# Where TensorE waits for transferred rows: on the scores that read them, or on fill products a slot or two ahead

## The chip, the cores and the metric

The kernel runs on one core of one Trainium2 chip. The metric is the device time of one execution in microseconds; lower is better. A time is the median of several runs, and one further execution was profiled.

## What is computed

An input x of 2048 tokens by 512 features is normalised, goes through sliding-window attention (32 heads of 16 features, each query sees itself and the 255 keys before it) and through an MLP with a gate, and the two are joined:

```python
xn = layernorm(x)
qkv = xn @ wqkv                                   # 32 heads of 16
scores = (q @ k.T) * 16 ** -0.5, masked to 0 <= i - j < 256
s = (softmax(scores) @ v) @ wo
h = gelu(layernorm(xn) @ w1 + b1)                 # 1792 wide
g = silu(h @ w2 + b2)
out = x + s * g
```

Everything is in float32; products are built from a rounded high part and a low remainder of each operand, three products for one.

## The kernel before, in words

The attention part is a hand-written pipeline of **slots**. One slot t handles one block of 128 queries or keys of one group n of four heads; there are 8 groups of 16 blocks, so t runs from 0 to 127, with a few slots ahead of 0 for the start. A slot has two halves. In each, TensorE first makes the probabilities' scores of one pair of heads into the one tile `stb` (`prob_block`), which ScalarE then raises into `pt`; `stb` may be written again only when ScalarE has read it. Between the two halves stand other products: the scores of a block 12 slots ahead, used only for the row maxima (`max_block` into `xy`, `first_scores` into `zo`), the product of probabilities and values (`pv_step`, `zo<-pt,vt`), and **fill products**: single matmuls of other stages (`fb<-xnT,wqb` and the like) that the tables `fills` deal out to the slots.

Scores read `slots[n % 2]` (tiles `qk0`, `qk1`), which hold the query and key rows of a group in a layout that matmuls cannot write. So a fill stage computes 512 columns (a chunk c of group n) into the bank `fb`, ScalarE copies it to `pjr` and rounds it to `sh`, GpSimd subtracts for the low part, and SyncE's queue carries the rows into the slot tile: four transfers of `sh`, two of `pjr`, from group 2 on one more (`copy_rows`, called by `send`, `send_high` and `send_low` in `job_qk` and `pair_qk`). The row maxima of four blocks go the same way through HBM (`max_rows`; the last step, `bring_in`, is `qk<-mT_d`).

`tandem(t0, t1, one, two)` deals out the fill products of two such stages over slots t0 to t1, in pairs that sit on the two row halves of the array; each `unit` is one pair, and it returned nothing. `fill_in(t, half)` runs what is due in a half slot. All engines but SyncE keep program order, so what stands behind a waiting matmul on TensorE waits too. Which semaphores a matmul waits for was left to the tile framework: the first reader of a tile waits for all the transfers into it, so the first score of a chunk carried up to eight waits.

Of the kernel before, what the change touches and what calls it, by code (L numbers as in the profile page):

```python
# [9 lines left out]
F32 = mybir.dt.float32  # L10
# [8 lines left out]
P = 128  # L19
# [9 lines left out]
ORDER = mybir.DependencyInfo(mybir.DependencyClass.Sync, mybir.DependencyReason.DATA)  # L29
# [21 lines left out]
def mixer_kernel(ctx, tc, x, wqk, wv, wo, w1, b1, w2, b2, out):  # L51


    nc = SimpleNamespace(**{name: Ordered(tc, name) for name in ("tensor", "vector", "scalar", "gpsimd", "sync")})
# [16 lines left out]
        (eng or nc.scalar.copy)(dst_hi, src)  # L71
        nc.vector.tensor_sub(dst_lo, src, dst_hi.bitcast(F32))

    def copy_rows(dst, src):
        nc.sync.dma_start(dst.bitcast(F32), src.bitcast(F32))

    def load(pool, tag, src, name, shape=(P, 512)):
        t = pool.tile(list(shape), F32, tag=tag, name=name)
# [81 lines left out]
    def run(steps):  # L160
        for step in steps:
            step()
# [11 lines left out]
    slots = []  # L174
# [126 lines left out]
    def job_qk(n, c):  # L301

        box = []
        ops = [(kt, a, b) for kt in range(KT) for a, b in PASSES]
        if not n and c < 3:
            ops.sort(key=lambda o: o[2])
        sl = slice(512 * c, 512 * (c + 1))

        def mm(i):
            if i == 0:  # L310
                box.append(fill_bank() if n or c else xy[:, 0])
            kt, a, b = ops[i]
            nc.tensor.matmul(box[0], wqs[n][:, a, kt], big[:, b, kt, sl],
                             start=(i == 0), stop=(i == len(ops) - 1))

        def send(src, qk, tt):
            copy_rows(slots[n % 2][tt:P:4, qk, :, sl], src[64 * qk: 64 * qk + 64])

        def finish():
            hi = sgp.tile([P, 512], F32R, tag="sh", name=f"sh_{n}_{c}", bufs=2)  # L320
            raw = t2.tile([P, 512], F32, tag="t2", name=f"pjr_{n}_{c}")
            lo = raw.bitcast(F32R)
            src = raw if n else box[0]
            if n:
                nc.scalar.copy(raw, box[0])

            def high():
                nc.scalar.copy(hi, src)
                behind(now[0], send_high)

            def send_high():
                for qk, tt in ((1, 0), (0, 0), (1, 2), (0, 1)):
                    send(hi, qk, tt)

            def low():
                (nc.gpsimd if n else nc.vector).tensor_tensor(lo, src, hi.bitcast(F32), op=ALU.subtract)
                behind(now[0], send_low)

            def send_low():
                send(lo, 1, 1)  # L340
                send(lo, 0, 2)

            later(1 if n else 0, high)
            later(3 if n else 1, low)
        return [(216, mm, i) for i in range(len(ops))], finish
# [17 lines left out]
    def pair_qk(n, c):  # L363

        ops = [(kt, a, b) for kt in range(KT) for a, b in PASSES]
        sl = slice(512 * c, 512 * (c + 1))

        def mm(ps, i, r, **flags):
            kt, a, b = ops[i]
            return nc.tensor.matmul(ps, wqs[n][r, a, kt], big[r, b, kt, sl], **flags)  # L370

        def send(src, qk, tt):
            copy_rows(slots[n % 2][tt:P:4, qk, :, sl], src[64 * qk: 64 * qk + 64])

        def finish(ps, t, copy):
            hi = sgp.tile([P, 512], F32R, tag="sh", name=f"sh_{n}_{c}", bufs=2)
            raw = t2.tile([P, 512], F32, tag="t2", name=f"pjr_{n}_{c}")
            lo = raw.bitcast(F32R)
            copy(raw, ps)

            def send_high():
                if n >= 2:
                    copy_rows(slots[n % 2][3:P:32, 0, :, sl], slots[n % 2][7:P:32, 0, :, sl])
                for i, (qk, tt) in enumerate(((1, 0), (0, 0), (1, 2), (0, 1))):
                    send(hi, qk, tt)
                    if i == 1 and (n, c) in among:
                        among[n, c]()

            def send_low():
                send(lo, 1, 1)  # L390
                send(lo, 0, 2)


            free = t if (n, c) == (1, 2) else max(t + 1 + 2 * (c % 2), 16 * n - 28 + 4 * c)
            free += 2 * (t == 90)
            (behind if free == t else at)(free, nc.scalar.copy, hi, raw)
            behind(free, send_high)
            free = quiet(max(free, t + 1))
            at(free, lambda: nc.gpsimd.tensor_tensor(lo, raw, hi.bitcast(F32), op=ALU.subtract))
            behind(free, send_low)  # L400
        return 3 * KT, mm, finish
# [38 lines left out]
    def tandem(t0, t1, one, two, mid=None, back=None):  # L440

        n = one[0]
        lo, hi = slice(0, 64), slice(64, P)
        mid = mid or max(1, (t0 + t1 + 1) // 2)
        most = n // 4

        def places(slots, last):

            last = min(most, n // (len(slots) + 1)) if last else 0
            cuts = [(n - last) * k // len(slots) for k in range(len(slots) + 1)]
            out = []
            for t, a, b in zip(slots, cuts, cuts[1:]):
                ahead = min(b - a, 5 * n // 12) if t < 16 * NQ - LEAD else min(b - a, max(most, (b - a + 1) // 2))
                out += [(t, 0)] * ahead + [(t, 1)] * (b - a - ahead)
            return out + [(t1, 0)] * last

        first, second = places(range(t0, mid), False), places(range(back or mid, t1), True)
        for phase, where in enumerate((first, second)):  # L460
            for i in range(n):
                flags = dict(start=(phase == 0 and i == 0), stop=(phase == 1 and i == n - 1), skip_group_check=True)
                def unit(i=i, phase=phase, flags=flags):
                    made = ((two if phase == 0 else one)[1](fb[1 - phase], i, hi, **flags),
                            (one if phase == 0 else two)[1](fb[phase], i, lo, **flags))
                    if phase == 1 and i == 0 and t0 < 16 * NQ - LEAD:
                        for r in made:
                            tc.add_manual_dep(r.ins, outs["copy"].ins.name, ORDER, reason="the banks change rows")
                fills.setdefault(where[i], []).append((unit, ()))
        fills.setdefault((t1, 0), []).append((one[2], (fb[0], t1, nc.scalar.copy)))  # L470
        if t1 >= 16 * NQ - LEAD:
            fills[t1, 0].append((two[2], (fb[1], t1, nc.vector.tensor_copy)))
            return
        ends_pair.add(t1)

        def copy(dst, src):
            outs["second"] = nc.scalar.copy(dst, src)
        fills.setdefault((t1, 1), []).append((two[2], (fb[1], t1, copy)))
# [45 lines left out]
    def max_rows(n, c, t):  # L524

        mt = mts.pop((n, c))
        mh = small.tile([P, 2, 2, 2, 4], F32R, tag="mh", name=f"mh_{n}_{c}")
        apart = t >= 0
        eng = nc.gpsimd if apart else nc.vector
        eng.tensor_copy(mh[:, :, 0], mt)  # L530
        eng.tensor_tensor(mh[:, :, 1], mt, mh[:, :, 0].bitcast(F32), op=ALU.subtract)
        mT = small.tile([P, 32], F32, tag="mT", name=f"mT_{n}_{c}")

        def turn_rows():
            nc.vector.transpose(mT, mh.rearrange("p a l i b -> p (a l i b)").bitcast(F32))
        if apart:
            behind(t + 1, turn_rows)
        else:
            turn_rows()
        t += apart  # L540
        rows = mT_d[n, c]
        at(t + 1, nc.sync.dma_start, rows.rearrange("r (i t) -> i r t", i=4), mT)

        def bring_in():
            nc.sync.dma_start(slots[n % 2][3:P:32, 0, :, 512 * c: 512 * (c + 1)].bitcast(F32),
                              rows.rearrange("(h p b) t -> h p (b t)", h=4, p=2))
        if (n, c) == (6, 3):
            among[7, 3] = bring_in
        else:
            behind(t + 2, bring_in)  # L550
# [168 lines left out]
    n, raw = raws["qk"]  # L719
# [99 lines left out]
    def ones():  # L819
# [4 lines left out]
           -10: [ln3[0][0], ln3[1][0], ln3[0][1], ln3[1][1], ln3[0][2], ln3[1][2]],  # L824
           -9: [ln3[2][0], ln3[3][0], ln3[2][1], ln3[3][1], ln3[2][2], ln3[3][2]]}

    def fill_in(t, half):
        now[:] = t, half
        run(delayed.pop((t, half), ()))
        for fn, args in fills.get((t, half), ()):  # L830
            fn(*args)

    end = 16 * NQ
    for t in range(-16, end + 1):
# [62 lines left out]
    for f in range(6, NF, 2):  # L897
        t = gp.tile([P, 2, 512], F32, tag="ohl", name=f"hr_{f}", bufs=4)
# [206 lines left out]
    for c in range(2):  # L1105
        accs = open_accs(c)
        gs, os_, hs, wanted = {}, [], {}, []
        made = ready if c == 0 else {}
# [21 lines left out]
        for i in range(NF + 1):  # L1130
# [35 lines left out]
            k = i - o_from  # L1166
# [136 lines left out]
    for i in range(NF):  # L1303
# [12 lines left out]
        if 4 <= i < 8:  # L1316
            wanted = load_o(3, i - 4)
# [34 lines left out]
```

## Time and profile before

| | |
|---|---|
| median of 3 runs | 739.98 us (739.8 to 740.8) |
| the profiled execution's own time | 740.08 us |
| its span, as the profile counts it | 738.4 us |
| TensorE busy | 725.1 us |
| TensorE's weight loads busy | 587.2 us |
| ScalarE, VectorE, GpSimd busy | 444.0, 509.8, 297.6 us |
| mean granted TensorE clock | 0.999 |

Slot 0 begins at about 62 us of the span and slot 127 ends at about 420 us. Every operation is recorded by one helper, so all rows have the line L43 and are told apart by their tiles. PE is TensorE's matmuls, PEld its weight loads, SPq the issue of a transfer on SyncE's queue. Each matmul has a weight load just ahead of it; a matmul's semaphore wait is held by that weight load, so the start of a weight load (PEld row) is where a wait is seen. The timeline merges neighbours of one kind: "x4" in a row is four of them, and the duration is that of the four together. Instructions that only wait for semaphores are in no row; time that they take shows as "issue".

### The profile page before, as it was taken

The numbers are of one execution on the slowest core, as the hardware profiler recorded it, in microseconds if no ns is written. First come the engines' busy times: TensorE is split into PE (matmuls) and PEld (weight loads), VectorE is DVE, ScalarE is ACT, GpSimd is POOL, SyncE is SP. The second block draws the span as 40 slices with busy tenths as digits, with TensorE's granted clock in tenths as the row PEclk, the third lists the DMA queues.
The fourth block names the chain that finished last, engine by engine and source line by source line (L and its number), as shares of the span: only waits on it lengthen the run. The fifth ranks groups of instructions, "written<-read, shape, count | busy, mean of one in ns | idle before, by whom it ended". The sixth has DMA issues, their size and how long they took to land.

```text
span 738.4 us, 18757 instructions
## 1 busy us (share of the span) xinstructions
PE 725.1 (98%) x7360; PEld 587.2 (80%) x7360; DVE 509.8 (69%) x790; ACT 444.0 (60%) x744; POOL 297.6 (40%) x644
## 2 busy tenths in 40 slices
PE   8999999999999999999999999999999999999997
PEld 7886777777778888777776688888888888888886
DVE  7886677877766678887772577656667855667733
ACT  7757767877777676778877756443644734541001
POOL 7413757867666555767867600120102000001102
PEclk9999999999999999999999999999999999999999
DMA  8633356766555524747724397657452322163711
GB/s 292 194 69 77 83 144 165 198 162 186 146 145 148 158 66 153 177 127 184 206 84 148 106 323 194 178 134 206 108 110 100 111 76 86 60 183 118 228 40 57
DMA packets 84697, 105.71 MB, mean 143 GB/s; under 512 B 37312, under 2 KB 37568, under 8 KB 84608
## 3 DMA queue, kind: packets, MB, share of 16 engines
q1 hardware_dynamic: 84608, 104.51, 50.7%
q8 instruction: 58, 0.95, 0.5%
q14 instruction: 31, 0.25, 0.1%
HBM read 54.53 MB, written 32.77 MB: 118 GB/s over the span
## 4 chain that ended last, share of the span: by engine, by line
PE 91%; ACT 4%; DVE 2%; POOL 1%; DMA 1%; issue 1%; SPq 0%; DVEq 0%; ACTq 0%
PE acc L43 21%; PE fb L43 19%; PE zo L43 13%; PE stb L43 9%; PE p L43 9%; PE s L43 6%; PE h L43 6%; PE xy L43 5%; ACT pt L43 4%; PE pv L43 3%; POOL pt L43 1%; DVE xy L43 1%; DMA x<-in_x_dram 1%; DVE mt L43 0%; PE tr L43 0%
## 5 line engine op out<-in xcount | busy, mean ns | idle before, releaser
L43 POOL TENSOR_SCALAR_AFFINE_SELECT pt<-pt 128x256 f32<-128x256 f32 x480 | 193.0, 426 | 128.9 <-ACT pt L43 126.1
L43 ACT ACTIVATE pt<-stb 128x768 f32<-128x768 f32 (+1 forms) x244 | 188.7, 773 | 52.6 <-PE stb L43 46.3
L43 DVE TENSOR_REDUCE mt<-xy 128x4 f32<-128x1024 f32 (+1 forms) x128 | 152.6, 1192 | 4.4
L43 DVE COPY_PREDICATED xy<-upper,zo 128x512 f32<-128x512 int32 x112 | 77.8, 694 | 70.4 <-PE xy L43 63.0
L43 POOL TENSOR_TENSOR xo<-xo,gated 128x512 f32<-128x512 f32 x15 | 19.9, 1328 | 235.0 <-DVE gated L43 195.6
L43 PE MATMUL fb<-xnT,wqb 64*128 64x512 f32 (+1 forms) x684 | 104.6, 397 | 0.0
L43 PE MATMUL zo<-pt,vt 128*17 128x128 f32 x2880 | 103.7, 275 | 0.3 <-POOL pt L43 0.3
L43 PE MATMUL stb<-qk 64*128 64x384 f32 (+1 forms) x488 | 94.6, 383 | 6.0 <-ACT pt L43 4.3
L43 PE MATMUL acc<-w,gh 128*128 128x512 f32 x320 | 98.4, 389 | 0.0
L43 PEld LDWEIGHTS stb<-qk 64*128 64x128 f32 x488 | 45.8, 183 | 48.3 <-ACT pt L43 41.4
L43 PEld LDWEIGHTS zo<-pt,vt 128*17 128x17 f32 x2880 | 67.5, 97 | 15.6 <-issue 5.0
L43 PEld LDWEIGHTS fb<-xnT,wqb 64*128 64x128 f32 (+1 forms) x684 | 64.8, 185 | 9.5 <-issue 0.6
L43 PEld LDWEIGHTS acc<-w,gh 128*128 128x128 f32 x320 | 60.1, 188 | 12.4
L43 PE MATMUL acc<-w,gl 128*128 128x512 f32 x160 | 62.2, 389 | 0.0
L43 PE MATMUL xy<-qk 64*128 64x256 f32 (+2 forms) x536 | 58.3, 291 | 0.2 <-DVE mt L43 0.2
L43 PEld LDWEIGHTS xy<-qk 64*128 64x128 f32 x536 | 46.6, 185 | 6.8 <-issue 3.2
L43 ACT COPY oraw<-zo 128x128 f32<-128x128 f32 x108 | 28.7, 266 | 30.8 <-PE zo L43 20.4
L43 ACT ACTIVATE gated<-acc 128x512 f32<-128x512 f32 x16 | 8.7, 595 | 59.3 <-DVE acc L43 59.3
L43 PE MATMUL s<-wos,ohl 128*128 128x512 f32 (+1 forms) x204 | 44.3, 376 | 0.0
L43 PEld LDWEIGHTS s<-wos,ohl 128*128 128x128 f32 x204 | 36.8, 188 | 7.1
L43 ACT COPY p<-p 128x512 f32<-128x512 f32 x21 | 12.3, 585 | 48.6 <-PE p L43 41.4
L43 PEld LDWEIGHTS zo<-qk 64*128 64x128 f32 x448 | 37.5, 185 | 4.8 <-DVE xy L43 1.8
(190 smaller groups left out, 1238.9 us busy)
## 6 DMA issues: line engine op xcount, KB each, us to landing
qk<-sh SPq DMA_DIRECT2D x128, 128.0 KB
qk<-pjr SPq DMA_DIRECT2D x64, 128.0 KB
oT_d<-oraw SPq DMA_DIRECT2D x32, 256.0 KB
w_d<-in_w_dram SPq DMA_DIRECT2D x14, 512.0 KB
x<-in_x_dram SPq DMA_DIRECT2D x16, 256.0 KB
or<-oT_d SPq DMA_DIRECT2D x16, 256.0 KB
w<-rden_d SPq DMA_DIRECT2D x16, 256.0 KB
xo<-in_x_dram SPq DMA_DIRECT2D x16, 256.0 KB
```

Source lines behind the costliest of these rows:

```text
L43: r = issue(*args, **kwargs)
```

## The change

No instruction of any engine is added, removed or moved. What changes is which matmuls wait for the transfers. `copy_rows` and `bring_in` now remember the transfers by chunk; `unit` returns its two matmuls (in the first pair of a phase, none); and `fill_in` keeps a list `wanted` of transfers that the coming scores read, and lets each following fill product depend on one of them:

```diff
+    brought = {}
+
+    def copy_rows(dst, src, key=None):
+        r = nc.sync.dma_start(dst.bitcast(F32), src.bitcast(F32))
+        brought.setdefault(key, []).append(r)
...
+                        return ()
+                    return made if i else ()
...
+    wanted = []
+
     def fill_in(t, half):
         now[:] = t, half
         run(delayed.pop((t, half), ()))
+        if half == 0 and t >= 3:
+            k, s = t + 1, (t + 14) // 4
+            if k % 16 == 0 or k % 4 == 2 and k % 16 < 14:
+                wanted[:0] = brought.get(("max", k // 16, (k % 16 + 2) // 4), [])
+            if t % 4 == 2 + (t < 18):
+                wanted[:] = wanted[:1] + brought.get(("qk", s // 4, s % 4), [])
         for fn, args in fills.get((t, half), ()):
-            fn(*args)
+            for r in fn(*args) or ():
+                if wanted:
+                    tc.add_manual_dep(r.ins, wanted.pop(0).ins.name, ORDER, reason="the next slot reads these rows")
```

The rows of a chunk are waited for one slot ahead of their first score while t is below 18 and two slots ahead from there on; maxima one slot ahead. In all, 193 fill products take one wait each; scores that waited for transfers and for an engine keep only the engine.

On TensorE in slot 3, ahead of the first scores of group 1 (DMAHW0 to DMAHW7 are the counters of transfers; here the four transfers of `sh` and, on DMAHW7 and DMAHW0, the two of `pjr`):

```order
-L43 MATMUL fb_109<-xnT,wqb_709 128x512
-L43 MATMUL fb_108<-xnT,wqb_709 128x512
-L43 MATMUL fb_109<-xnT,wqb_709 128x512
-L43 MATMUL fb_108<-xnT,wqb_709 128x512
-L43 MATMUL fb_109<-xnT,wqb_709 128x512
-L43 MATMUL fb_108<-xnT,wqb_709 128x512
+L43 MATMUL fb_109<-xnT,wqb_709 128x512 [waits DMAHW3_49]
+L43 MATMUL fb_108<-xnT,wqb_709 128x512 [waits DMAHW4_49]
+L43 MATMUL fb_109<-xnT,wqb_709 128x512 [waits DMAHW5_49]
+L43 MATMUL fb_108<-xnT,wqb_709 128x512 [waits DMAHW6_49]
+L43 MATMUL fb_109<-xnT,wqb_709 128x512 [waits DMAHW7_49]
+L43 MATMUL fb_108<-xnT,wqb_709 128x512 [waits DMAHW0_49]
```

Three of the four pairs of fill products of that half slot now wait, the last of them for the two transfers of low rows. In slot 4 the first score loses those waits:

```order
 L43 MATMUL stb<-qk_91 128x384 [waits Activation_49]
 L43 MATMUL stb<-qk_91 128x384
-L43 MATMUL xy<-qk_695 128x128 [waits DMAHW5_49,DMAHW4_49,DMAHW6_49,DMAHW3_49,DMAHW7_49,DMAHW0_49,DVE_49]
+L43 MATMUL xy<-qk_695 128x128 [waits DVE_49]
 L43 MATMUL xy<-qk_695 128x128 x3
```

Six waits went from the score to products that stand one `stb` half and one `pv_step` ahead of it. The same happens to chunk 2 of group 1, on TensorE in slot 11, ahead of slot 12:

```order
-L43 MATMUL fb_109<-xnT,wqb_1111 128x512
-L43 MATMUL fb_108<-xnT,wqb_1111 128x512
-L43 MATMUL fb_109<-xnT,wqb_1111 128x512
-L43 MATMUL fb_108<-xnT,wqb_1111 128x512
-L43 MATMUL fb_109<-xnT,wqb_1111 128x512
-L43 MATMUL fb_108<-xnT,wqb_1111 128x512
+L43 MATMUL fb_109<-xnT,wqb_1111 128x512 [waits DMAHW2_49]
+L43 MATMUL fb_108<-xnT,wqb_1111 128x512 [waits DMAHW3_49]
+L43 MATMUL fb_109<-xnT,wqb_1111 128x512 [waits DMAHW4_49]
+L43 MATMUL fb_108<-xnT,wqb_1111 128x512 [waits DMAHW5_49]
+L43 MATMUL fb_109<-xnT,wqb_1111 128x512 [waits DMAHW7_49]
+L43 MATMUL fb_108<-xnT,wqb_1111 128x512 [waits DMAHW0_49]
```

Here it is the first three of four pairs that wait, the third for the low rows; the first score of slot 12 had carried the same six.

More of the change, by code (lines that the diff above doesn't have):

```diff
@@ L72, in split @@
         nc.vector.tensor_sub(dst_lo, src, dst_hi.bitcast(F32))
-    def copy_rows(dst, src):
-        nc.sync.dma_start(dst.bitcast(F32), src.bitcast(F32))
+    brought = {}
+    def copy_rows(dst, src, key=None):
+        r = nc.sync.dma_start(dst.bitcast(F32), src.bitcast(F32))
+        brought.setdefault(key, []).append(r)
     def load(pool, tag, src, name, shape=(P, 512)):
@@ L316, in send @@
         def send(src, qk, tt):
-            copy_rows(slots[n % 2][tt:P:4, qk, :, sl], src[64 * qk: 64 * qk + 64])
+            copy_rows(slots[n % 2][tt:P:4, qk, :, sl], src[64 * qk: 64 * qk + 64], ("qk", n, c))
         def finish():
@@ L372, in send @@
         def send(src, qk, tt):
-            copy_rows(slots[n % 2][tt:P:4, qk, :, sl], src[64 * qk: 64 * qk + 64])
+            copy_rows(slots[n % 2][tt:P:4, qk, :, sl], src[64 * qk: 64 * qk + 64], ("qk", n, c))
         def finish(ps, t, copy):
@@ L382, in send_high @@
                 if n >= 2:
-                    copy_rows(slots[n % 2][3:P:32, 0, :, sl], slots[n % 2][7:P:32, 0, :, sl])
+                    copy_rows(slots[n % 2][3:P:32, 0, :, sl], slots[n % 2][7:P:32, 0, :, sl], ("qk", n, c))
                 for i, (qk, tt) in enumerate(((1, 0), (0, 0), (1, 2), (0, 1))):
@@ L544, in bring_in @@
         def bring_in():
-            nc.sync.dma_start(slots[n % 2][3:P:32, 0, :, 512 * c: 512 * (c + 1)].bitcast(F32),
-                              rows.rearrange("(h p b) t -> h p (b t)", h=4, p=2))
+            brought["max", n, c] = [nc.sync.dma_start(slots[n % 2][3:P:32, 0, :, 512 * c: 512 * (c + 1)].bitcast(F32),
+                                                      rows.rearrange("(h p b) t -> h p (b t)", h=4, p=2))]
         if (n, c) == (6, 3):
```

## The prediction

> **What bounds the kernel now.** The first lines of the page say how much TensorE works, the groups say what its weight loads wait for, and the view of waits of the weight loads says how often.
>
> ```profile
> span 738.4 us, 18757 instructions
> PE 725.1 (98%) x7360; PEld 587.2 (80%) x7360; DVE 509.8 (69%) x790; ACT 444.0 (60%) x744; POOL 297.6 (40%) x644
> L43 PEld LDWEIGHTS stb<-qk 64*128 64x128 f32 x488 | 45.8, 183 | 48.3 <-ACT pt L43 41.4
> PEld stb L43 <- ACT pt L43: 41.4, 142, 0.7
> PEld zo L43 <- issue: 6.4, 22, 0.4
> PEld xy L43 <- issue: 3.2, 14, 0.4
> PEld stb L43 <- issue: 2.7, 12, 0.4
> ```
>
> TensorE is busy 98% of the span, so nothing but its own time can move the end. But in the attention slots the busy share hides a ring: the one tile `stb` goes from TensorE to ScalarE and back, and 142 of its rewrites (out of 244 pairs) waited for ScalarE, 0.29 us on average. Where that wait is, TensorE work ahead of it has cover: it may start later by as much at no cost. The last three rows are weight loads that started late with nothing in the profile to blame. Instructions that only wait stand in no row, so this is where a score with many waits would show. All three together, 12.3 us, are more than any removal of waits can give back.
>
> **What the removed waits cost.** Heads of chunks, each from one `stb` load to the next, all weight loads:
>
> ```profile
> 120.10 0.19 PEld L43 LDWEIGHTS stb<-qk 64*128 64x128 f32 x2 [0.47 <-ACT pt L43]
> 120.49 0.33 PEld L43 LDWEIGHTS xy<-qk 64*128 64x128 f32 x4 [0.21 <-DVE oraw L43]
> 121.75 0.21 PEld L43 LDWEIGHTS stb<-qk 64*128 64x128 f32 x2
> 123.28 0.18 PEld L43 LDWEIGHTS stb<-qk 64*128 64x128 f32 x2 [0.21 <-ACT pt L43]
> 123.39 0.36 PEld L43 LDWEIGHTS xy<-qk 64*128 64x128 f32 x4
> 124.72 0.19 PEld L43 LDWEIGHTS stb<-qk 64*128 64x128 f32 x2
> 166.07 0.19 PEld L43 LDWEIGHTS stb<-qk 64*128 64x128 f32 x2 [0.47 <-ACT pt L43]
> 166.37 0.33 PEld L43 LDWEIGHTS xy<-qk 64*128 64x128 f32 x4
> 167.43 0.19 PEld L43 LDWEIGHTS stb<-qk 64*128 64x128 f32 x2
> 209.81 0.19 PEld L43 LDWEIGHTS stb<-qk 64*128 64x128 f32 x2 [0.41 <-ACT pt L43]
> 211.36 0.22 PEld L43 LDWEIGHTS stb<-qk 64*128 64x128 f32 x2
> 217.26 0.19 PEld L43 LDWEIGHTS stb<-qk 64*128 64x128 f32 x2
> 218.83 0.18 PEld L43 LDWEIGHTS stb<-qk 64*128 64x128 f32 x2 [0.21 <-ACT pt L43]
> 220.42 0.19 PEld L43 LDWEIGHTS stb<-qk 64*128 64x128 f32 x2
> 221.99 0.19 PEld L43 LDWEIGHTS stb<-qk 64*128 64x128 f32 x2 [0.21 <-ACT pt L43]
> ```
>
> At 123.28 the score `xy` carries one wait and its loads follow 0.11 us after those of `stb`. At 120.10 (first score of group 2, eight waits) they follow after 0.39 us, at 166.07 (group 3, seven waits) after 0.30. So waits on one instruction cost its queue 0.2 to 0.3 us, though what they wait for has long landed. Whether the slot pays is seen in the `stb` loads. With the same four scores and ten fill products, 120.10 to 121.75 is 1.65 us and 123.28 to 124.72 is 1.44: 0.21 paid. 209.81 to 211.36 (group 4) is 1.55 against the same 1.44: 0.11. At 166.07 there are eight fill products, and the half takes 1.36, which is what the ring takes anyway: nothing paid. There are eight such heads, one to each of groups 1 to 7 and one in slot 12. The other chunks spread their waits over three scores: the half from 220.42 holds one with four waits (`zo`) and takes 1.57 us, as does the half from 217.26 with the same products and no such waits. I take **0.8 us gained** in all (0.21, 0.11, about 0.2 in slot 4 with the half behind it, about 0.3 in slot 12, the rest nothing). Bounds: nothing, and 8 times 0.21, or 1.7.
>
> The Trainium skill, "Perfetto Trace Analysis", section "Identifying Dependency Chains", says that an instruction which waits on several engines may get EventSemaphore instructions ahead of it. That agrees with the 0.39 against 0.11 us; it names no price, so the sum stays as it is.
>
> What the waits cost in their new place when the transfer has landed: one wait to a product is held by the product's own weight load. The fill products of slot 3 below hold one (for ScalarE) in eight, those of slot 11 none, and both rows show 0.78 us for eight loads: I take zero, with 0.05 either way for all.
>
> **What the added waits cost when it has not.** The first place is slot 3. Weight loads, the issue of the two transfers of low rows, and the row of what the DMA engines moved from 72 to 75 us, in forty slices of 0.075 us:
>
> ```profile
> 71.72 1.17 SPq L43 DMA_DIRECT2D qk<-pjr  x2
> 72.04 0.78 PEld L43 LDWEIGHTS fb<-xnT,wqb 64*128 64x128 f32 x8
> 72.99 0.19 PEld L43 LDWEIGHTS stb<-qk 64*128 64x128 f32 x2 [0.17 <-ACT pt L43]
> 74.34 0.19 PEld L43 LDWEIGHTS stb<-qk 64*128 64x128 f32 x2 [0.41 <-ACT pt L43]
> 74.70 0.33 PEld L43 LDWEIGHTS xy<-qk 64*128 64x128 f32 x4 [0.18 <-issue]
> GB/s 0 0 0 0 0 0 0 0 0 0 0 0 218 164 355 82 355 82 300 109 164 191 246 246 191 246 137 191 137 82 0 0 0 0 0 191 191 300 109 300
> ```
>
> The last of the four pairs starts at 72.04 + 0.78 - 0.19 = 72.63. The low rows are still on their way: packets move until the thirtieth slice, that is 74.25, and the score that waits for them starts at 74.70. So they land between 74.25 and 74.70. I take 74.65, because the pause from 74.25 to 74.63 ahead of the next transfer looks like the time to completion, and because the score left at once. Then the pair waits 2.02 us; it stood 0.17 us ahead of need (the wait of `stb` at 72.99), so **1.9 us** are paid, with bounds 1.4 and 2.1. Behind the pair are queued `stb`, thereby ScalarE's exponentials, GpSimd's masks, and everything later: the ring at 1.35 us a half has nothing with which to catch up.
>
> The second place is slot 11, with DMA activity from 94 to 98 us in slices of 0.1 us, and the row of that window's queues that isn't the kernel's:
>
> ```profile
> 92.53 1.17 SPq L43 DMA_DIRECT2D qk<-pjr  x2
> 94.53 0.78 PEld L43 LDWEIGHTS fb<-xnT,wqb 64*128 64x128 f32 x8
> 95.48 0.19 PEld L43 LDWEIGHTS stb<-qk 64*128 64x128 f32 x2 [0.17 <-ACT pt L43]
> 97.23 0.33 PEld L43 LDWEIGHTS xy<-qk 64*128 64x128 f32 x4 [0.21 <-issue]
> DMA  9496897985798999639201011100100689699299
> q8 instruction: 1, 0.02, 2.2%
> ```
>
> Here the third pair holds the wait: about 94.53 + 0.78 - 0.19 - 0.23 = 94.89, a pair taking 0.23 us. The row is dense until 96.0, then single packets trickle until 96.9, and the score starts at 97.23. In the window an instruction fetch of 2.2% of 16 engines' 4 us, or 1.4 us, held one DMA engine, so the transfer's share on that engine came late. Landing is between 95.1 (the issue's end, 93.70, plus the 1.4 us from 72.89 to 74.25 of the first place) and 97.23; I take 97.15, since the score started then. The pair waits 2.26 us, less about 0.13 of cover: **2.1 us** paid, with bounds 0.1 and 2.2.
>
> A third place, group 6, is on the edge:
>
> ```profile
> 295.94 1.19 SPq L43 DMA_DIRECT2D qk<-pjr  x2
> 297.48 0.77 PEld L43 LDWEIGHTS fb<-xnT,wqb 64*128 64x128 f32 x8
> 298.39 0.19 PEld L43 LDWEIGHTS stb<-qk 64*128 64x128 f32 x2
> ```
>
> The last pair is at 297.48 + 0.77 - 0.19 = 298.06 and waits for the first transfer of low rows only, issued at 295.94, which by the first place (second issue at about 71.72 + 0.58 = 72.30, landed at 74.65) lands 2.35 us later, at 298.29, by packets perhaps a little sooner: I take 298.25. With 0.05 for the release and 0.1 of cover that is **0.15 us**, with bounds 0 and 0.4. The other chunks are brought in further ahead of their products, so I put nothing down for them.
>
> A rule speaks against the change: the Trainium skill, "DMA: Bandwidth & Descriptors", section "Rules for kernel authors", wants the semaphore waited on late, so that the fixed part of a transfer overlaps with compute. The two places above agree with it. By the rule alone every group would pay; by the rows only those do whose transfers are still under way, and the sum is made from the rows.
>
> **The sum**, against the profiled execution's own 740.08 us, which is 0.1 us above the median of 739.98: 740.08 + 1.9 + 2.1 + 0.15 - 0.8 = 743.4 us, 743.3 beside the median.
>
> **The rivals.** (a) Only the first wait is paid. The late landing in slot 11 hangs on one instruction fetch; with wait instructions gone from TensorE's stream the fetch may come at another moment, and the landing back at about 95.2 to 95.8. Then that term is 0.1 to 0.7: 741.3 to 742.0. For it: the trickle and the fetch. Against it: only a few instructions leave ahead of slot 11, so the fetch should fall within a few tenths of the same place.
>
> (b) The other side: the wait instructions are worth more than the two stalls. The place is the weight loads of `stb`, `xy` and `zo` that are late by "issue", 12.3 us; it would show if that lateness sat on the path also where I saw it covered, for instance by delaying VectorE's maxima and so the slots behind. It decides from a gain of 4.2 us on, a third of those rows; with half of them the time is 740.08 + 4.15 - 6.15 = 738.1. Against it: the heads at 166.07 and 209.81 give 0 and 0.11.
>
> (c) More products than three stall, since each moved wait has lost one or two slots of lead: the maxima, too, are now waited for a slot earlier. Two further stalls of the third place's upper size, 0.4, with the full bounds of the first two (2.1 and 2.2) and no gain give 740.08 + 4.3 + 0.4 + 0.8 = 745.6; a middle case is 744.5.
>
> **How the numbers follow.** Forecast 743.4 us against the profiled time, **743.3** against the median, chance 0.62; (a) 0.18; (b) 0.12; (c) 0.08. The range leaves out (b) and the far end of (c): 741.2 to 744.6. A measurement of this kernel tells about 0.2% from no change, 1.5 us. Slower by more than that is the forecast, (c) and most of (a): 0.85. Within it lie the low end of (a) and the part of (b) with a gain between 2.7 and 5.6 us: 0.11. Faster is the rest of (b): 0.04.
>
> **What would show it.** In the profile of the changed kernel, the fill products of slot 3 should be broken ahead of the last pair, with about 2 us of idle weight loads put down to issue or to the transfer, and the next `stb` at about 74.9 instead of 72.99. Slot 11 should show the same ahead of the third pair, some 2 us later in the span than before. The score after 120.10 should follow its `stb` by 0.11 us instead of 0.39, and group 2's first half slot should shrink to 1.44. If slot 3 is not broken, the low rows land earlier than I read and the forecast is wrong; if it is, and the end comes no later, the ring has slack that I did not see.

## The result, and the profile after

The changed kernel took **744.9 us** (median of 6 runs, 744.03 to 747.85) against 740.35 us for the kernel before (six runs, the three from above among them): a ratio of 1.0071, with an interval of 1.0056 to 1.0086. The forecast was 743.3 us with a range of 741.2 to 744.6; direction and place were right, the size was too small by 1.6 us. Set against its own before, it was 3.3 us forecast and 4.55 measured; the other 0.4 us is the median of before, 739.98 in three runs and 740.35 in six. The profiled execution is one of the two longest: 747.55 us, span 745.8 us, mean granted clock 0.993.

First the waits of TensorE's weight loads after the change (total us, times, longest):

```profile
...
PEld zo L43 <- issue: 7.7, 25, 0.5
PEld fb L43 <- DMA qk<-pjr: 4.8, 4, 2.4
PEld stb L43 <- issue: 3.1, 13, 0.4
PEld xy L43 <- issue: 2.5, 11, 0.4
...
PEld fb L43 <- DMA qk<-sh: 0.2, 1, 0.2
```

Two rows are new: four times a fill product stood still for low rows, 4.8 us in all, and once for high rows, 0.2 us, in slot 82. The three rows "issue" together are 13.3 us, before 12.3: no lateness has gone. Now the two places in the timeline of weight loads, slot 3 and then slot 11:

```profile
71.42 0.19 PEld L43 LDWEIGHTS stb<-qk 64*128 64x128 f32 x2 [0.21 <-ACT pjr L43]
...
73.81 0.18 PEld L43 LDWEIGHTS fb<-xnT,wqb 64*128 64x128 f32 x1 [1.44 <-DMA qk<-pjr]
74.47 0.18 PEld L43 LDWEIGHTS fb<-xnT,wqb 64*128 64x128 f32 x1 [0.48 <-DMA qk<-pjr]
74.48 0.29 PEld L43 LDWEIGHTS stb<-qk 64*128 64x128 f32 x2
76.05 0.18 PEld L43 LDWEIGHTS stb<-qk 64*128 64x128 f32 x2 [0.40 <-ACT pt L43]
76.55 1.40 PEld L43 LDWEIGHTS fb<-xnT,wqb 64*128 64x128 f32 x8
78.04 0.33 PEld L43 LDWEIGHTS stb<-qk 64*128 64x128 f32 x2
80.06 0.18 PEld L43 LDWEIGHTS stb<-qk 64*128 64x128 f32 x2 [0.21 <-ACT pt L43]
...
96.93 0.18 PEld L43 LDWEIGHTS stb<-qk 64*128 64x128 f32 x2 [0.23 <-ACT pt L43]
...
100.29 0.50 PEld L43 LDWEIGHTS fb<-xnT,wqb 64*128 64x128 f32 x3 [2.42 <-DMA qk<-pjr]
100.46 0.75 PEld L43 LDWEIGHTS stb<-qk 64*128 64x128 f32 x2
103.17 0.29 PEld L43 LDWEIGHTS stb<-qk 64*128 64x128 f32 x2 [0.41 <-issue]
105.79 0.33 PEld L43 LDWEIGHTS stb<-qk 64*128 64x128 f32 x2
107.76 0.19 PEld L43 LDWEIGHTS stb<-qk 64*128 64x128 f32 x2 [0.21 <-ACT pt L43]
```

The stalls are where they were forecast: at the last pair in slot 3 (1.44 us ahead of its first product and 0.48 ahead of its second) and at the third pair in slot 11 (2.42, ahead of its second product). The next `stb` comes at 74.48. But something follows that was not forecast: the half slots **behind** a stall are long too. After 74.48 they take 1.57, 1.99 and 2.02 us, after 100.46 they take 2.71, 2.62 and 1.97. (The first half behind a stall is a little long at any clock, 1.57 and 1.70 us in the profile of e8 below; the rest is not.) The row at 76.55 shows what it is: eight loads took 1.40 us, where the same eight took 0.80 before:

```profile
74.92 0.80 PEld L43 LDWEIGHTS fb<-xnT,wqb 64*128 64x128 f32 x8
```

The windows of that execution (behind each engine's busy time stand the granted clock, the DMA share and GB/s) say so directly:

```profile
74.00:76.00 2.00, 1.75 (x28) 0.86 (x27) 0.16 (x1) 0.81 (x1) 0.00 (x0) 1.00 0.75 162
76.00:78.00 2.00, 1.95 (x12) 1.72 (x14) 1.07 (x2) 1.08 (x2) 1.68 (x6) 0.58 0.48 101
78.00:80.00 2.00, 2.00 (x30) 1.10 (x26) 0.50 (x2) 0.81 (x1) 1.55 (x3) 0.57 0.00 0
...
98.00:100.00 2.00, 0.30 (x3) 0.00 (x0) 1.64 (x2) 0.74 (x2) 0.77 (x2) 1.00 0.36 116
100.00:102.00 2.00, 1.71 (x13) 1.03 (x17) 0.00 (x0) 0.14 (x1) 0.00 (x0) 0.55 0.93 202
102.00:104.00 2.00, 2.00 (x30) 1.46 (x24) 0.00 (x0) 1.04 (x3) 1.13 (x4) 0.50 0.73 197
104.00:106.00 2.00, 2.00 (x16) 1.70 (x14) 1.26 (x2) 0.71 (x1) 1.22 (x3) 0.50 0.00 0
106.00:108.00 2.00, 2.00 (x34) 1.57 (x34) 0.77 (x2) 0.86 (x2) 1.13 (x2) 0.74 0.00 0
```

The granted clock is 1.00 during the stall and falls to half two to four microseconds after its start, when TensorE is at work again or just about to be. Nothing of the kind is in the kernel before:

```profile
72.00:80.00 8.00, 7.75 (x126) 5.66 (x122) 5.52 (x8) 6.46 (x11) 5.89 (x16) 1.00 0.53 117
94.00:102.00 8.00, 7.88 (x118) 6.19 (x110) 5.34 (x8) 5.44 (x10) 6.04 (x15) 1.00 0.71 176
```

So the theory to test (A): the change costs its stalls, and the idle time in them can make the granted clock fall, which is paid on top. Its rivals: (B) moved waits cost something at every product, also where the transfer has long landed; (C) the clock falls in this stretch for another reason; (D) it falls by chance, whatever the idle time.

### The profile page after: what moved, and what is told of

Its sections match the earlier page's. It is cut to its first block, busy times and chain, and to the rows that moved or that the text cites. A ratio compares the mean times of both kernels' runs of the same rounds, so it can differ in the third digit from the quotient of the medians.

```text
span 745.8 us, 18635 instructions
## 1 busy us (share of the span) xinstructions
PE 729.0 (98%) x7360; PEld 588.9 (79%) x7360; DVE 510.0 (68%) x790; ACT 443.9 (60%) x744; POOL 297.8 (40%) x644
## 4 chain that ended last, share of the span: by engine, by line
PE 83%; ACT 5%; issue 4%; POOL 3%; DVE 2%; DMA 2%; SPq 0%; ACTq 0%; DVEq 0%; POOLq 0%
PE acc L43 20%; PE fb L43 17%; PE zo L43 12%; PE p L43 9%; PE stb L43 8%; PE s L43 6%; PE h L43 6%; PE xy L43 4%; ACT pt L43 3%; POOL pt L43 2%; DMA qk<-pjr 1%; PE pv L43 1%; ACT x L43 1%; DVE xy L43 1%; DVE mt L43 0%
## 5 line engine op out<-in xcount | busy, mean ns | idle before, releaser
L43 PE MATMUL fb<-xnT,wqb 64*128 64x512 f32 (+1 forms) x684 | 108.4, 405 | 3.3 <-DMA qk<-pjr 3.3
L43 PE MATMUL stb<-qk 64*128 64x384 f32 (+1 forms) x488 | 96.6, 388 | 5.5 <-ACT pt L43 4.2
L43 ACT COPY p<-p 128x512 f32<-128x512 f32 x21 | 12.3, 585 | 48.6 <-PE p L43 41.2
```

What stands on the lines that cost most here:

```text
L43: r = issue(*args, **kwargs)
```

## The experiments

Ten kernels in three sessions after that first measurement (e1 to e4, e5 to e8, e9 and e10); those of a session ran on one chip with the kernel before. All times are medians, "falls" are the executions with a lower mean granted clock (0.997 or less). Of the 58 executions of the kernel before in these sessions none is below 0.998.

| run | what is moved | us | before | ratio (95% interval) | falls |
|---|---|---|---|---|---|
| e1 | all but the waits of the two places | 739.97 | 740.07 | 0.9997 (0.9988 to 1.0006) | 0 of 11 |
| e2 | slot 3 alone | 742.10 | 740.07 | 1.0030 (1.0020 to 1.0039) | 2 of 9 |
| e3 | slot 11 alone | 741.92 | 740.07 | 1.0027 (1.0017 to 1.0037) | 1 of 9 |
| e4 | all, 8 idle products in each stall | 744.22 | 740.07 | 1.0055 (1.0043 to 1.0068) | 0 of 5 |
| e5 | all, 3 idle products in each stall | 743.75 | 740.14 | 1.0046 (1.0033 to 1.0059) | 0 of 5 |
| e6 | slot 3 alone, longer idle piece | 743.94 | 740.14 | 1.0049 (1.0037 to 1.0061) | 5 of 5 |
| e7 | all but three places | 739.85 | 740.14 | 0.9994 (0.9985 to 1.0002) | 0 of 11 |
| e8 | all (the change again) | 743.79 | 740.14 | 1.0054 (1.0041 to 1.0067) | 3 of 6 |
| e9 | slot 3 alone, idle in one piece | 742.25 | 740.36 | 1.0024 (1.0014 to 1.0035) | 1 of 8 |
| e10 | slot 3 alone, shorter idle piece | 741.56 | 740.36 | 1.0017 (1.0008 to 1.0025) | 0 of 11 |

### e1: the change without the two places

```diff
-            if t % 4 == 2 + (t < 18):
+            if t % 4 == 2 + (t < 18) and s not in (4, 6):
```

> The change as it is, but the waits for the rows of chunks (1, 0) and (1, 2) stay with the scores; all other moved waits are kept. Theory A (the loss is two stalls, in slots 3 and 11, and the lower granted clock behind them; the other moved waits gain a little): 739.6 to 740.1 us against 740.35, since 0.3 to 0.7 us came back at the heads of groups in the trace; granted clock 1.00 in every window from 60 to 130 us. Rival B (moved waits cost something wherever they are, a few hundredths of a microsecond at each of some 60 products): 741.5 us or more. Rival C (the clock falls in this stretch for another reason, such as the changed order of instructions): clock under 0.95 somewhere between 70 and 125 us although no product waits there, and 742 us or more.

Measured 739.97 us, clock 0.999 to 1.000 in every execution. The loss is gone with the two places, although some 180 products still carry moved waits: B and C fall. The small gain is within the interval. One stall was left, which was also in the change: in slot 82 the last product waited for the first transfer of group 6.

### e2 and e3: one place alone

```diff
-            if k % 16 == 0 or k % 4 == 2 and k % 16 < 14:
+            if False:
...
-            if t % 4 == 2 + (t < 18):
+            if t == 3:
```

> Only the waits of slot 3 are moved, those for the rows of chunk (1, 0); all others as before the change. Theory A: a stall of 1.7 us in slot 3 and then up to 1.4 us more from a lower clock, less some 0.1: 742.0 to 743.4 us, with the clock near 0.8 from 72 to 80 us and 1.00 from 94 us on. Rival C (the clock falls in slot 11's stretch for another reason): a lower clock from 94 to 102 us here too. If the stall alone counted: 742.0.

e3 has `t == 11` in the last line.

> Only the waits of slot 11 are moved, those for the rows of chunk (1, 2); all others as before the change. Theory A: a stall of about 2.1 us in slot 11 and then up to 2.8 us from a lower clock, less some 0.3: 742.2 to 745.0 us, with the clock at 1.00 until 95 us and near 0.9 from 95 to 103. Rival C: a lower clock from 72 to 80 us here too. If the instruction fetch near 94 us comes at another moment, the stall shrinks to a few tenths and the time to 740.5.

The two differences to before, 2.03 and 1.85 us, add to 3.9. Most executions show the stall alone. In e2 seven take 741.57 to 742.19 us at a clock of 0.999 to 1.000, and two take 743.43 and 743.50 at 0.997. In e3 eight take 741.75 to 742.11 and one takes 743.39 at 0.996. So one fall costs about 1.5 us, and it does not come each time. e3 came out 0.3 us below the band that I had given it, since I had counted part of a fall in. Their profiled executions kept their clock at 1.00 from 60 to 420 us. The 0.998 of e3's comes from the end of its span: behind the last matmul the window from 738 to 740 us stands at 0.50. Several profiles have such a piece, so 0.998 alone does not tell whether the clock fell earlier.

### e4 and e5: TensorE kept at work during the stalls

```diff
+            if t in (3, 11) and half == 0 and len(wanted) == 2:
+                for _ in range(8):
+                    nc.tensor.matmul(zo[:, 0, 384:512], ident, ident, start=True, stop=True)
```

> The change as it is, with eight idle products of the identity with itself (128 x 128, into columns of a PSUM tile that nobody reads) placed right ahead of the pair that waits in slot 3 and in slot 11, so that TensorE works during much of each stall. They add work where there was idle time, so the end should not move by them. Theory A (the clock falls because TensorE idles for about 2 us): the idle stretch falls under about 1 us, the clock stays at 1.00, and the time is the forecast's stalls without the clock's part, 743.2 to 743.8 us, every round alike. If the clock has nothing to do with the idle time: 744.5 to 745.5, with the clock near 0.8 and 0.9 as in the change.

The clock stayed at 0.999 to 1.000 in all five executions, but the time was 744.22, above the band. The weight loads of e4 tell why:

```profile
72.11 0.54 PEld L43 LDWEIGHTS fb<-xnT,wqb 64*128 64x128 f32 x6
73.23 1.86 PEld L43 LDWEIGHTS zo<-ident 128*128 128x128 f32 x16 [0.58 <-DVE xy L43]
...
75.32 0.19 PEld L43 LDWEIGHTS stb<-qk 64*128 64x128 f32 x2
```

The idle products first waited 0.58 us for VectorE, which still read their tile, and then ran past the landing: the waiting pair shows no wait any more, and `stb` comes 3.62 us after the one at 71.70 rather than about 3.06. The run answers for the clock and mixes up the time, so e5 has three products (`range(3)`):

> The change with three idle products instead of eight ahead of the waiting pair in slots 3 and 11. With eight the clock stayed at 1.00 in all five executions, but they ended later than the transfer (1.86 us of loads from 73.23 in slot 3, half slots of 3.62 and 3.84 us instead of 3.06 and 3.14 to 3.52 in the other runs), which cost 0.5 us at each place. Three take 0.7 us, so they end ahead of the landing. Theory A (idle time lowers the clock; without that the change costs its stalls alone): half slots of about 3.1 and 3.2 us, clock 1.00, 743.4 to 743.9 us, all executions within 0.6 us. If idle products do not protect the clock in themselves, or the idle rest of 0.6 us and more is already enough: some executions 1.5 us or more above the others, median 744.5 or more.

```profile
73.18 0.74 PEld L43 LDWEIGHTS zo<-ident 128*128 128x128 f32 x6 [0.58 <-DVE xy L43]
...
74.71 0.18 PEld L43 LDWEIGHTS fb<-xnT,wqb 64*128 64x128 f32 x1 [0.48 <-DMA qk<-pjr]
74.72 0.29 PEld L43 LDWEIGHTS stb<-qk 64*128 64x128 f32 x2
```

Now the idle products end ahead of the landing, and the stall is as long as in the change (71.65 to 74.72, 3.07 us) but partly filled. The clock stayed up in all five, and the five took 742.96 to 744.05 us (a spread of 1.1, more than the 0.6 that I had written). Their median, 743.75, is 3.61 above before. That is what the change costs **when the clock does not fall**. The run does not separate it from e8, whose median is the same; it shows the size of the part without the clock.

### e8: the change once more

> The change itself once more, beside the three others on the same chip, for the spread of its clock. Theory A: the executions stand on steps, about 743.7 us without a fall of the clock, about 745 with one and 747.5 with a fall behind both stalls, with the lower clock in the same order; the median near 744.9. If the profiled execution's clock was an accident: all near 743.7.

Median 743.79 on this chip, 1.1 us below the 744.9 that I had written and inside the range of the prediction, which the first measurement of the same program was not. The steps are there, though less even than I had written: 742.59 and 743.80 us at a clock of 1.000, 743.47 at 0.999, 743.78 at 0.997, 745.41 at 0.996, 746.50 at 0.995. In the first measurement it was 745.03 at 0.999, 744.03 and 744.32 at 0.998, 744.78 at 0.997, and 747.55 and 747.85 at 0.993. Apart from 743.80, 743.78 and 745.03 a lower clock goes with a longer time. Of the twelve the median is 744.55. The profiled execution of this run kept its clock, and so it can be laid beside the first one; the program is the same:

```profile
71.53 0.19 PEld L43 LDWEIGHTS stb<-qk 64*128 64x128 f32 x2 [0.21 <-ACT pjr L43]
74.60 0.29 PEld L43 LDWEIGHTS stb<-qk 64*128 64x128 f32 x2
78.86 0.19 PEld L43 LDWEIGHTS stb<-qk 64*128 64x128 f32 x2 [0.41 <-ACT pt L43]
95.76 0.18 PEld L43 LDWEIGHTS stb<-qk 64*128 64x128 f32 x2 [0.23 <-ACT pt L43]
98.81 0.29 PEld L43 LDWEIGHTS fb<-xnT,wqb 64*128 64x128 f32 x3 [2.11 <-DMA qk<-pjr]
98.92 0.42 PEld L43 LDWEIGHTS stb<-qk 64*128 64x128 f32 x2
103.52 0.19 PEld L43 LDWEIGHTS stb<-qk 64*128 64x128 f32 x2 [0.23 <-ACT pt L43]
```

The same four half slots each of the kernel before:

```profile
71.64 0.19 PEld L43 LDWEIGHTS stb<-qk 64*128 64x128 f32 x2 [0.21 <-ACT pjr L43]
77.21 0.19 PEld L43 LDWEIGHTS stb<-qk 64*128 64x128 f32 x2 [0.40 <-ACT pt L43]
94.13 0.19 PEld L43 LDWEIGHTS stb<-qk 64*128 64x128 f32 x2 [0.23 <-ACT pt L43]
99.98 0.19 PEld L43 LDWEIGHTS stb<-qk 64*128 64x128 f32 x2 [0.23 <-ACT pt L43]
```

From slot 3's `stb` on, four half slots took 5.57 us before, 7.33 in e8 and 8.64 (71.42 to 80.06) in the first execution: 1.76 us are the stall and 1.31 the clock. At slot 11 it was 5.85, 7.76 and 10.83 us (96.93 to 107.76): 1.91 and 3.07. Of the 3.07, 0.31 is a longer stall (2.42 against 2.11 us, at a clock of 1.00), which leaves 2.76 for the clock. So in that execution the two stalls cost 3.98 us and the clock 4.07.

### e6, e9 and e10: how long the idle time must be

Slot 3 alone each time. e6 puts all six waits on one product, the first that takes a wait (in the second of the four pairs, since the first pair of a phase takes none), e9 the last two waits on one product, and e10 leaves the last wait at the score:

```diff
-                if wanted:
+                while wanted:
```

```diff
-                if wanted:
+                for _ in wanted[:2 if len(wanted) == 2 else 1]:
```

```diff
-                wanted[:] = wanted[:1] + brought.get(("qk", s // 4, s % 4), [])
+                wanted[:] = wanted[:1] + brought.get(("qk", s // 4, s % 4), [])[:-1]
```

> Slot 3 alone, with all six waits on the first product of the first pair, so that TensorE idles in one piece from about 71.9 to 74.6 us, 2.6 us instead of 1.4 and 0.5 in two pieces. The stall alone gives 740.07 + 2.5 = 742.6 us. Theory A (the longer TensorE idles, the more often the clock falls behind it): most executions fall, against two of nine with 1.9 us of idle time, and the median is 743.8 to 745.0 with a clock of 0.995 to 0.998. Rival D (the fall comes by chance, whatever the length of the idle time): again about two of nine, and a median of 742.4 to 742.8.

> Slot 3 alone as before (742.1 us, clock fallen in two of nine executions), but the last two waits stand on one product, so that TensorE's idle time of 1.4 and 0.5 us with a product between is one piece of about 2.1 us. The stall alone gives 741.9 to 742.2 us. If the length of one idle piece decides whether the clock falls (none of 2.5 us let it stand, pieces of 1.4 to 2.1 us mostly did): more executions fall than two of nine, but not all, each 1.4 us longer with a clock near 0.997. If the idle share of a longer stretch decides: again about two of nine.

> Slot 3 alone, with the wait for the last transfer of low rows left at the score that needs it: five waits moved, one stays. TensorE then idles in one piece of 1.4 us and no more, and the first half slot is longer by about 1.05 us, which the score's own wait for the last transfer no longer adds to. 740.07 + 1.1 = 741.0 to 741.3 us, and by theory A the clock never falls: clock 0.999 to 1.000 in every execution, none 1 us above the others. If 1.4 us were enough for a fall: some executions at 0.997 and 742.5.

The stalled product in each profile (e6, e9, e10):

```profile
74.99 0.53 PEld L43 LDWEIGHTS fb<-xnT,wqb 64*128 64x128 f32 x6 [2.46 <-DMA qk<-pjr]
```

```profile
74.73 0.19 PEld L43 LDWEIGHTS fb<-xnT,wqb 64*128 64x128 f32 x2 [2.10 <-DMA qk<-pjr]
```

```profile
74.27 0.19 PEld L43 LDWEIGHTS fb<-xnT,wqb 64*128 64x128 f32 x2 [1.44 <-DMA qk<-pjr]
```

With 2.46 us the clock fell in all five executions (0.997 each, 743.72 to 744.01 us). With 2.10 us in one piece it fell in one of eight (743.31 at 0.997), much as with the 1.44 and 0.48 of e2. With 1.44 us it fell in none of eleven. One execution of e10 took 742.61 us at a clock of 1.000, so about a microsecond can come from elsewhere too; and e10's median was 0.3 us above its band, which was counted from 740.07 us for the kernel before, where the runs beside e10 have 740.36. That it falls whatever the idle time (D) is out: none of eleven, four of 26 (e2, e3, e9), five of five. The weight lies on the five of five; none of eleven against four of 26 could be chance. The runs being compared lie on three chips (e2 and e3; e6; e9 and e10), and a part of the chip in these counts is not excluded. That gluing the pieces together would matter was not borne out. The windows of e6:

```profile
74.00:76.00 2.00, 1.01 (x8) 0.67 (x8) 0.67 (x1) 0.00 (x0) 0.06 (x1) 0.95 0.74 162
76.00:78.00 2.00, 2.00 (x28) 1.21 (x28) 0.00 (x0) 1.00 (x2) 0.80 (x3) 0.50 0.71 152
78.00:80.00 2.00, 2.00 (x16) 1.56 (x14) 1.28 (x2) 0.89 (x2) 1.10 (x5) 0.69 0.00 0
```

At half clock a window of 2 us with mean clock c spent 2 x (1 - c) / 0.5 us. That makes 0.2, 2.0 and 1.24 us here, 3.4 in all.

### e7: a version without any stall

```diff
-            if t % 4 == 2 + (t < 18):
+            if t % 4 == 2 + (t < 18) and s not in (4, 6, 24):
```

> The change without the three sets of moved waits that a product stood still for: rows of chunks (1, 0), (1, 2) and (6, 0); the other moved waits are kept. No product then waits for a transfer for more than 0.1 us. Theory A: the shifts of the half slots against before show only gains, about 0.1 us at each of four or five heads, no loss at 298 us (it was 0.28 net), 739.5 to 739.8 us. If the moved waits have a cost that the other runs hid: 740.1 or more.

739.85 us, 0.05 above the band and 0.9994 of before with 1 inside the interval: a gain of 0.3 us is likely and not shown. Its trace shows where it would come from, first at the heads of groups 2 and 4:

```profile
120.40 0.18 PEld L43 LDWEIGHTS stb<-qk 64*128 64x128 f32 x2 [0.47 <-ACT pt L43]
120.51 0.36 PEld L43 LDWEIGHTS xy<-qk 64*128 64x128 f32 x4
121.92 0.19 PEld L43 LDWEIGHTS stb<-qk 64*128 64x128 f32 x2
...
209.90 0.19 PEld L43 LDWEIGHTS stb<-qk 64*128 64x128 f32 x2 [0.40 <-ACT pt L43]
211.33 0.19 PEld L43 LDWEIGHTS stb<-qk 64*128 64x128 f32 x2
```

The scores follow their `stb` by 0.11 us where it was 0.39 and 0.30, and the halves take 1.52 and 1.43 us instead of 1.65 and 1.55: gains of 0.13 and 0.12. A third half, from the `stb` at 349.75 to the one at 351.09, takes 1.34 us, where before (349.95 to 351.40) it was 1.45: 0.11. Part of this was hidden in that execution: the score of slot 12, which kept its waits, left 0.66 us behind its `stb` (at 97.54) against 0.40 before, which points to rows that landed later. No version here is shown to beat the kernel before.

## Why the prediction was too low

**The stalls: right.** The pair, the transfer and the size were as forecast. Together with what slots 4 and 12 gained, I had 1.9 - 0.2 and 2.1 - 0.3 us, or 3.5; e8 shows 1.76 and 1.91, or 3.67. The next `stb` was to come at 74.9 and came at 74.48, with a slot that began 0.22 us earlier than before.

**The third place: too small.** In slot 82 I had 0.15 us with an upper bound of 0.4. The row of e8:

```profile
302.03 0.18 PEld L43 LDWEIGHTS fb<-xnT,wqb 64*128 64x128 f32 x1 [0.47 <-DMA qk<-pjr]
```

From the `stb` at 300.24 to the one at 309.25 it is 9.01 us, before (297.04 to 305.71) it was 8.67: 0.34 us lost, net. The net lies within the bounds, the stall does not: the two halves at it are 0.44 and 0.19 us longer, and the last half of the stretch, behind the freed score of group 6, is 0.27 shorter (1.40 against 1.67).

**The removed waits: about right.** At the heads of groups I had 0.21 and 0.11 us; e7 gives 0.13 and 0.12, and 0.11 at a place that I had counted as nothing. The 0.27 behind slot 82 is in the 0.34 above; e7, where those waits were not moved, has 1.62 there, but whether the freed score or the stall ahead of it brings the gain the runs do not separate. My 1.44 us for group 2's first half was too short; it takes 1.52.

**The step that failed** is the sentence behind the first stall, "the ring at 1.35 us a half has nothing with which to catch up". It took the pace behind a stall for that of before, so a stall cost its own length and nothing else. The runs showed a pace of 2.0 to 2.7 us a half for a few half slots, because TensorE's granted clock can fall to half behind about 2 us of idle time or more. Without that the sum is good: 740.08 + 1.76 + 1.91 + 0.34 - 0.36 = 743.7 us (0.36 being the 0.13, 0.12 and 0.11), and e5, where the clock never fell, has 743.75 (the profiled execution of e8, from which the stalls are taken, has 743.47); the forecast was 743.3. The median of the first measurement lies 1.2 us higher, and the fall alone accounts for 1.1 to 1.6 us where it comes once (e2, e3, e9) and 4.1 where it came behind both stalls. How often it comes is chance as far as these runs show: e8's median, with three falls in six executions as well, has no such surplus. The page of before showed a clock of 0.999 and no idle piece of that size inside the attention, so no row of it priced the effect; but it was open to ask what the clock does behind the 2 us that I was adding, and I put down no term and no bound for it.

**The rivals.** (a) The instruction fetch still lay in the window of slot 11 after the change (95 to 101 us):

```profile
q8 instruction: 1, 0.02, 1.9%
```

1.9% of 16 engines' 6 us is 1.8 us on one DMA engine, and the second wait was paid in full. (b) The rows "issue" did not shrink, 13.3 us after the change and 12.6 in e7 (6.5, 2.7 and 3.4), against 12.3 before. (c) gave a time near the measured one, 744.5 to 745.6, by luck, for a reason that was not the one: no further products stalled but those of slot 82, for 0.18 and 0.47 us in the first execution.

**What stays open.** The same program came to a clock of 0.997 or less in three of six executions of the first measurement, twice to 0.993, and in three of six of e8, where the lowest was 0.995. What decides this at about 2 us of idle time no run here shows. Nor do the runs show the least idle time behind which the clock falls.

## What to carry to other kernels

A wait put on an earlier instruction is free only if the transfer has landed by then, so compare the landing with the new place, one transfer at a time, as was done here. Where a stall of about 2 us or more on TensorE results, add what the granted clock may lose behind it: here 1.1 to 2.8 us on top of 2, in some executions and not in others, so look at the spread of times and clocks, not at one profile. Freeing an instruction of six to eight waits whose events had long come was worth 0.11 to 0.13 us at the three places where it showed by itself.

## What the runs showed of the hardware

The falls that a profile caught lasted one length or twice that. By the formula under e6, the first execution spent 1.68 + 1.72 = 3.4 us at half clock behind slot 3 and 1.8 + 2.0 + 2.0 + 1.04 = 6.8 us behind slot 11, twice as much; e6 spent 3.4. The same rows of the first execution give the moments: the clock fell at 78 - 1.68 = 76.32 us and rose at 79.72, fell again at 100.2 and rose at 107.04. The distances between them, 3.40, 20.48 and 6.84 us, are one, six and two times 3.41, so all four lie on one grid that ran on between the stalls.

The Trainium skill, "TensorE: Matmul & The Clock Gate", section "Part 1: The HAM clock gate (the "warmup" mystery)", has the same length, a window of about 3.4 us that runs freely and is not started by the kernel, and a clock that is either whole or half. The durations and the grid here agree with it, and a free-running window would explain why one program falls in some executions only; that link is argued, not shown, and the place of the idle time in the window is not the whole of it. Counted back from the clock's fall in the idle end of e9's profile, at 740.27 us, by 195 lengths of 20.48 / 6 us, the window from 71.26 to 74.67 us held 2.0 of its 2.10 us of stall, and the clock stayed up; in the first execution the window from 72.91 to 76.32 us held 1.4 us of the stall, and it fell. The page's rule on how long TensorE must idle, a whole such window, does not agree: 2.46 us of idle weight loads (2.1 us between matmuls) were enough in five executions of five, and about 2 us, in one piece or two, in four of 26, so the measurement decides.
